# Splitting the shuffles of a long convolution into two transfers on two queues, in an H3 block with a token MLP

## The chip, the cores and the metric

The kernel runs on one core of one Trainium2 chip. The number that counts is the device time of one execution, in microseconds. Of the kernel before, three executions took 178.93, 179.75 and 180.01 us; the median is 179.75 us. A further execution, taken with the profiler, has its own time, and it is the one that the tables below describe.

The engines are TensorE (PE: matmuls and transposes, with a separate stream PEld for loading the stationary operand), VectorE (DVE), ScalarE (ACT), GpSimd (POOL) and SyncE (SP). Matmul results land in PSUM, which has eight banks here; everything else lives in SBUF, in 128 partitions. A transfer (DMA) is issued by an instruction on an engine's queue, here SP's, POOL's and a few on ACT's, and is carried out beside the engines.

## The reference

With S = 2048 positions, D = 448 channels and F = 1792 hidden units, all in bf16:

```python
h  = x + A(layernorm(x), k, v, shift_k, ssm_k, ssm_D)     # x is A_q
h2 = h + MLP(layernorm(h), w1, b1, w2, b2)

def A(q, k, v, shift_k, ssm_k, ssm_D):
    kv = shift_conv(k, shift_k) * v         # 4 taps, causal, along the positions
    y  = irfft(rfft(pad(kv)) * rfft(pad(ssm_k)))[:2048]    # along the positions, length 4096
    return q * (y + kv * ssm_D)

def MLP(x, w1, b1, w2, b2):                 # mixes positions, not channels
    u = gelu(einsum("bsd,sf->bdf", x, w1) + b1)
    return einsum("bdf,fs->bds", u, w2).transpose(0, 2, 1) + b2
```

So there is a layernorm of x, a product kv, a causal convolution of kv with a filter as long as the sequence, a gate, a second layernorm and a two-layer MLP over the 2048 positions.

## The kernel before

**Layout.** Position s is 16*q + r: q (0 to 127) lies on the partitions, r (0 to 15) in the free dimension beside the 448 channels. A tensor of the whole sequence is 128 partitions of 16 x 448 bf16 elements.

**The convolution** is done by discrete Fourier transforms written as matmuls, each transform in two stages, because a stage mixes either the partitions or the free index r. "k" stands for the filter, "u" for kv:

- *Transposes and kv* (L947, L1006 to L1028, L973, L988). The filter is transposed by PE, kv is made by PE with diagonal matrices (L973; the diagonals come from L932 on DVE, which waits for a copy L925 on POOL) and a product on DVE (L988). The tables of sines start with an angle computation on DVE, POOL and ACT (L809 to L855, with L812 and L825 on DVE and L835, L839 on POOL).
- *Stage 1* (L1040, function emit_stage1, called for k and then for u). For i in 0..3 and jh in 0..3 eight matmuls with a 128x32 stationary operand fill two PSUM banks; the result, 128 partitions x 896, is copied ("evacuated") to a slot of a ring of four buffers, by L1048 or L1050 on ACT or DVE. One slot holds one i, four jh.
- *Shuffle* (L1056). After every second jh the two finished quarters of a slot are moved between partitions, into TK or TU: source partition a + 4m + k goes to target partition a + i + 4m, so that four source partitions end side by side in one target partition. This is a DMA from SBUF to SBUF. In all there are 4 x 2 pairs for k and as many for u.
- *Stage 2* (L1075, emit_stage2), per index jj in 0..7 two blocks of 4 matmuls, each block evacuated by the helper evac (L719 and L720 on ACT, L722 and L723 on DVE; L720 and L723 are the scaled copies for k, L719 and L722 the plain ones).
- *Products* (L1108 on DVE, 16 of 128x1792) and *first inverse stage* (L1120, evacuated by L719 or L722). The first product waits for every shuffle of u, because its result lies in the memory of the ring.
- *Shuffle back* (L1144, and L1133 for the last pair), from TU to TZ: one transfer of 112 source partitions on POOL and one of 16 on SP per index; for the last pair on POOL, SP and ACT.
- *Second inverse stage* (L1240, per r) with a gate on DVE or ACT: L1249/L1251/L1259/L1269 form h from the result, the row statistics of x and x. Four transposes of a table ("ct", L1089) run between; dummy matmuls (L1154) too.

**Row statistics of x** are made on the side: bn_stats and bn_aggr on DVE (L1180, L1182), two small steps per pair of rows on POOL (L1185, L1188), normalised rows for r below 4 (L1197, L1200, then L1210 on ACT or L1212 on DVE). x itself is loaded (L896) into the ring's memory after all shuffles of u.

**The rest.** The second layernorm's statistics (L1275, L1287, L1297 to L1311) and its application (L1318 on DVE) give Q, row by row. The MLP's first layer is 112 matmuls L1365 (seven column blocks at once over 16 r, as Q comes) and 112 matmuls L1375, each block followed by a gelu (L1355 on ACT); the second layer is 16 groups of 14 matmuls (L1387), each added to h by L1390 on DVE and written out. The weights are loaded on SP (L1338, L1342, L1349) after the shuffles back.

**What sets the order.** Nothing is issued in the order of the text. Each helper call records an operation with its dependences. A list scheduler then lays the operations on the engines by a cost model, always taking, of those that are ready in the model and find a free buffer, the one with the lowest number; the numbers stand in the table WHEN, one for each step of each function (a step is one value of sch.t0). Operations that ACT or DVE could do are assigned by the table WHERE ("a" ACT, "d" DVE, "f" the scheduler's choice). PSUM banks and ring slots are also given out by this plan. The result is a fixed sequence for each engine and each queue: on the chip an engine waits at an instruction until its semaphores are there, and everything behind it on that engine waits too.

The lines that form one pair's shuffle, before:

```python
for q_, a, nu in (("pool", 0, 8), ("pool", 96, 8), ("sp", 32, 16)):
    shuf[tag].append(op(q_, lambda e, W, ...: e.dma_start(
        T[a + i:a + i + 4 * nu - 3:4]...,                      # nu target partitions, stride 4
        GR_(g.slots[0])[a:a + 4 * nu, jh - 1:jh + 1]...),      # 4 * nu source partitions
```

Of the kernel before, what the change touches and what calls it, by code (L numbers as in the profile page):

```python
# [9 lines left out]

ENGS = ("pe", "act", "dve", "pool", "sp")
WHEN = {
    "dummy": (283,),
    "tables": (138, 234, 288, 20, 81, 325, 139, 217,),
    "loads": (91, 107, 134, 143, 231, 216, 80, 297, 0, 238, 183, 285, 228, 299, 145,),
    "kv": (290, 148, 151, 174, 63, 282, 100, 192, 205, 47, 18, 112, 141, 45, 207, 160, 233,),
    "kT": (201, 13, 14, 175, 200, 130, 54, 53,),
    "k1": (132, 135, 152, 226, 122, 144, 165, 213, 68, 51, 154, 167, 89, 168, 262, 336,),
    "k2": (23, 150, 83, 97, 224, 227, 140, 153, 258, 248, 180, 195, 169, 219, 338, 235,),
    "u1": (71, 86, 116, 123, 46, 82, 176, 221, 117, 215, 261, 316, 173, 184, 277, 278,),  # L20
    "xload": (156, 298, 314, 302,),
    "bias": (75, 171,),
    "q": (271, 208, 318, 93, 268, 185, 279, 280, 264,),
    "u2": (133, 142, 220, 210, 241, 249, 64, 114, 159, 196, 137, 189, 1, 115, 252, 251,),
    "i1": (179, 121, 99, 3, 190, 96, 186, 149, 188, 240, 203, 202, 128, 92, 212, 95,),
    "ct": (36, 187, 87, 300,),
    "xn": (257, 17, 6, 222, 161, 317,),
    "w1a": (329, 239, 230, 55,),
    "w1b": (306,),
    "warm": (291, 307, 265, 27, 292, 147, 330, 320, 5, 304, 270, 38, 19, 315, 284, 62, 333, 327, 105, 118, 191, 295,  # L30
        324, 259, 56, 8, 332, 113, 236, 273, 206, 198, 182, 274,),
    "i2": (260, 69, 103, 39, 15, 31, 293, 28, 108, 242, 90, 84, 88, 331, 22, 197, 204, 33, 110, 237, 164, 323, 256,
        310, 73, 214, 223, 170, 44, 79, 157, 177, 16, 211, 328, 281, 131, 250, 4, 247, 158, 294, 109, 40, 29, 104,
        34, 243, 267, 129, 98, 287, 70, 178, 67, 162, 246, 120, 155, 2, 125, 11, 229, 42, 253, 272, 59, 124, 119,
        266, 12, 78, 194, 276, 127, 41, 313, 10, 102, 61, 255, 21, 37, 66, 24, 232, 199, 321, 312, 76, 308, 296, 52,
        111, 303, 163, 319, 58, 65, 339, 209, 26, 326, 337, 289, 85,),
    "w2": (146,),
    "mlp": (218, 57, 136, 126, 77, 30, 25, 48, 60, 9, 305, 72, 166, 245, 301, 172, 50, 181, 418, 419, 420, 421, 422,
        423, 424, 425, 426, 427, 428, 429, 430, 431, 432, 433, 434, 435, 436, 437, 438, 439,),
}  # L40
WHERE = {
    "kv": "ddaffffa",
    "kT": "fadfdddd",
    "k1": "fafaafaffaff",
    "k2": "dfdffadaafdafada",
    "u1": "fffaafadaaddafaa",
    "bias": "a",
    "u2": "fdaafafaaaaadafa",
    "i1": "affadfaaffdaffaf",
    "ct": "ffda",  # L50
    "xn": "aaff",
    "i2": "aaffaadafddf",
}


# [515 lines left out]
def _build(nc, A_q, A_k, A_v, A_shift_k, A_ssm_k, A_ssm_D, B_w1, B_b1, B_w2, B_b2, out):  # L571
# [54 lines left out]
    with ctx:  # L626
# [49 lines left out]
        def GR_(s):  # L676
            return view(o_GR[s], [R // 4, 2, D])
# [19 lines left out]
        def Ppair(b):  # L697
            s0, s1 = b.slots
            return PS[:, s0:s1 + 1, 0:D]
# [330 lines left out]
        def emit_stage1(src, o_src, T, o_T, tag):  # L1030
            shuf[tag] = []
            for i in range(R // 4):
                g = _Buf(gring)
                for jh in range(4):
                    sch.t0 = T_K1 + T_DK1 * (4 * i + jh) if tag == "k" else T_U1 + T_DU1 * (4 * i + jh)
                    b = _Buf(psum, 2)
                    c0 = 64 * (jh & 1) + 32 * (jh >> 1)
                    for x in range(2):
                        for q, r in enumerate((4 * i, 4 * i + 2, 4 * i + 1, 4 * i + 3)):
                            op("pe", lambda e, W, b=b, r=r, q=q, x=x, c0=c0: e.matmul(  # L1040
                                PS[32 * q:32 * q + 32, b.slots[x], 0:D], E[:, 2 * r + x, c0:c0 + 32], src[:, r, :],
                                start=True, stop=True, tile_position=(0, 32 * q)),
                               r=[(o_E + 512 * r + 256 * x + 2 * c0, 64), (o_src + r * DB, DB)], bw=[b], n=D, est=46.5, mode=1)

                    def fn(e, W, b=b, g=g, jh=jh, i=i):
                        dst = GR_(g.slots[0])[:, jh]
                        if tag == "k" and i == 0:
                            return e.tensor_tensor(out=dst, in0=Ppair(b), in1=DR.unsqueeze(1).broadcast_to([128, 2, D]),  # L1048
                                                   op=ALU.add)
                        return e.copy(out=dst, in_=Ppair(b)) if W == "act" else e.tensor_copy(out=dst, in_=Ppair(b))  # L1050
                    first = tag == "k" and i == 0
                    op("dve" if first else FX, fn, r=[(o_DR, DB)] if first else [], br=[b], bw=[g], n=2 * D, kind="psum")
                    if jh % 2 == 0:
                        continue
                    for q_, a, nu in (("pool", 0, 8), ("pool", 96, 8), ("sp", 32, 16)):
                        shuf[tag].append(op(q_, lambda e, W, g=g, i=i, a=a, nu=nu, jh=jh: e.dma_start(  # L1056
                            T[a + i:a + i + 4 * nu - 3:4].rearrange("p (j k) c d -> p j k c d", k=4)[:, :, jh - 1:jh + 1]
                            .rearrange("p j k c d -> p j (k c d)"),
                            GR_(g.slots[0])[a:a + 4 * nu, jh - 1:jh + 1].rearrange("p k c d -> p (k c d)")),
                           br=[g], w=[(o_T + (4 * j + jh - 1) * 2 * DB, 4 * DB, tag) for j in range(4)],  # L1060
                           dmab=4 * nu * 4 * DB, keng=nu, rate=350.0))
                wbufs.append(g)
# [296 lines left out]
        def emit_mlp():  # L1359
# [21 lines left out]
            for r in range(R):  # L1381
# [21 lines left out]

        PLAN = (("dummy", emit_dummy, ()), ("tables", emit_tables, ()), ("loads", emit_loads, ()), ("kv", emit_kv, ()), ("kT", emit_kT, ()),
                ("k1", emit_stage1, (KT, o_KT, TK, o_TK, "k")), ("k2", emit_stage2, (TK, o_TK, 1.0 / 2048.0)),
                ("u1", emit_stage1, (V, o_V, TU, o_TU, "u")),  
                ("xload", emit_xload, ()), ("bias", emit_bias, ()), ("q", emit_q, ()),
                ("u2", emit_stage2, (TU, o_TU, None)), ("i1", emit_products_i1, ()), ("ct", emit_ct, ()), ("xn", emit_xn, ()), ("w1a", emit_w1_load, (0,)), ("w1b", emit_w1_load, (1,)),
# [41 lines left out]
```

## Time and profile before

| what | value |
|---|---|
| three executions | 178.93, 179.75, 180.01 us (median 179.75) |
| the profiled execution | 178.13 us |
| its span, first to last instruction | 175.9 us |
| granted TensorE clock | 1.00 throughout |
| busy: PE, DVE, ACT, POOL | 166.1, 102.0, 92.2, 63.3 us |
| L1056 on POOL | 32 issues, 553 ns on average (median 544), 17.5 us |
| L1056 on SP | 16 issues, median 537 ns |
| L1056, from DMA to landing | 2.2 / 3.7 / 5.7 us (least, median, most) |
| L1144 on POOL | 14 issues, 588 ns on average, 8.2 us |

Some points in time of that execution, in microseconds from the start of the span:

| event | at |
|---|---|
| first L1040 of k | 13.72 |
| last stage-1 evacuation of k | 29.04 |
| last POOL shuffle of k issued, landed | 30.93, 35.90 |
| first L1075 of k | 35.99 |
| last stage-1 evacuation of u | 45.03 |
| last POOL shuffle of u issued, landed | 46.77, 50.79 |
| first, last L1108 | 50.89 start, 72.17 end |
| last evacuation of the first inverse stage | 75.17 |
| last POOL shuffle back (L1133) issued, landed | 76.30, 79.67 |
| first L1240 | 79.72 |
| first gate on DVE (L1269) | 80.31 |
| first, last L1318 | 84.80 start, 105.43 end |
| first L1365 | 85.59 |
| last matmul, end | 173.04, 175.9 |

How to read a profile: it is one execution. "Busy" is the time in which an engine had an instruction in work. The strip of 40 digits per engine shows the busy share in tenths for each fortieth of the span (4.4 us here). The chain is the sequence of work that ended last, followed back from the last instruction to whatever released it; a DMA piece there runs from the issue to the landing. A transfer's row gives the size and the median time from issue to landing. An engine's idle time matters only where the chain passes through it.

### The profile page before, as it was taken

The page shows a single profiled execution, that of the slowest core. Times are in us where ns is not written, and L with a number is a line of the kernel's source. Part 1 is how long each engine was busy: PE and PEld are TensorE (multiplying, and loading weights), DVE is VectorE, ACT ScalarE, POOL GpSimd, SP SyncE. Part 2 cuts the span into 40 slices and gives each one's busy share as a digit, 9 for nine tenths or more (in the row PEclk, how much of TensorE's full clock was granted, in tenths as well). Part 3 has the DMA queues.
Part 4 walks back from the last instruction along what each step waited for, and adds up shares of the span by engine and source line. Part 5 has one row for each costly group of instructions (what it writes and reads, how often), then busy time and mean ns, then how long its engine had stood idle before and what let it go on. Part 6 is the DMA issues. An engine that isn't in the chain of part 4 may idle for free.

```text
span 175.9 us, 3619 instructions
## 1 busy us (share of the span) xinstructions
PE 166.1 (94%) x1445; PEld 95.6 (54%) x1445; DVE 102.0 (58%) x189; ACT 92.2 (52%) x131; POOL 63.3 (36%) x157
## 2 busy tenths in 40 slices
PE   6999999879979999998999999999999999999994
PEld 2786745342323333644544455555557777777784
DVE  6995696848999999998998860000001231331331
ACT  3799958888979999966982656412120000000000
POOL 8576628670600643894888760000000000000000
PEclk9999999999999999999999999999999999999999
DMA  5999855992849386569999999910000111011111
GB/s 174 416 334 332 268 165 201 325 352 71 250 98 383 110 214 198 167 179 390 383 396 405 421 419 417 419 77 0 0 4 0 52 52 52 16 40 52 52 52 52
DMA packets 15444, 35.13 MB, mean 200 GB/s; under 512 B 3820, under 2 KB 9484, under 8 KB 15428
## 3 DMA queue, kind: packets, MB, share of 16 engines
q1 hardware_dynamic: 12164, 28.00, 43.4%
q0 software_dynamic: 3072, 6.80, 12.6%
q8 instruction: 11, 0.18, 0.4%
q10 hardware_dynamic: 192, 0.11, 0.2%
q14 instruction: 5, 0.04, 0.1%
HBM read 22.05 MB, written 1.84 MB: 136 GB/s over the span
## 4 chain that ended last, share of the span: by engine, by line
PE 68%; ACT 10%; POOL 7%; DMA 7%; DVE 4%; issue 2%; DVEq 0%; POOLq 0%
PE ps L1387 24%; PE ps L1375 12%; PE ps L1365 9%; ACT arena L719 8%; DMA arena<-arena 7%; PE ps L1040 4%; PE ps L1006 3%; POOL arena L1056 3%; PE ps L947 3%; PE ps L1240 3%; PE ps L1075 2%; PE ps L1019 2%; PE ps L973 2%; PE ps L1120 2%; DVE arena L1259 1%
## 5 line engine op out<-in xcount | busy, mean ns | idle before, releaser
L1390 DVE SCALAR_TENSOR_TENSOR arena<-ps,arena 128x448 bf16<-128x448 f32 (+2 forms) x17 | 11.1, 656 | 57.4 <-PE ps L1387 57.4
L1387 PE MATMUL ps<-arena 128*128 128x448 bf16 (+2 forms) x238 | 42.7, 342 | 0.0
L1387 PEld LDWEIGHTS ps<-arena 128*128 128x128 bf16 x238 | 33.3, 145 | 9.5
L719 ACT CAST arena<-ps 128x896 bf16<-128x896 f32 (+1 forms) x29 | 23.4, 948 | 1.2 <-PE ps L1075 1.1
L1365 PE MATMUL ps<-arena 128*128 128x448 bf16 x112 | 22.9, 353 | 0.4 <-DVE arena L1318 0.4
L1056 POOL DMA_DIRECT2D arena<-arena x32 | 17.5, 553 | 14.1 <-ACT arena L1050 12.9
L1050 ACT CAST arena<-ps 128x896 bf16<-128x896 f32 x24 | 20.3, 919 | 3.8 <-PE ps L1040 3.5
L1375 PE MATMUL ps<-arena 128*128 128x448 bf16 x112 | 21.8, 353 | 0.0
L1075 PE MATMUL ps<-arena 128*64 128x448 bf16 x128 | 15.8, 360 | 3.4 <-DMA arena<-arena 1.8
L1355 ACT ACTIVATE arena<-ps,arena 128x448 bf16<-128x448 f32 x14 | 8.6, 633 | 19.4 <-PE ps L1375 17.7
L1108 DVE TENSOR_TENSOR arena<-arena 128x1792 bf16<-128x1792 bf16 x16 | 16.7, 1080 | 0.2
L1365 PEld LDWEIGHTS ps<-arena 128*128 128x128 bf16 x112 | 10.6, 98 | 11.5 <-DVE arena L1318 2.5
L1375 PEld LDWEIGHTS ps<-arena 128*128 128x128 bf16 x112 | 10.9, 98 | 10.2
L1040 PE MATMUL ps<-arena 128*32 128x448 bf16 x256 | 15.3, 356 | 0.4 <-DVE arena L988 0.3
L1120 PE MATMUL ps<-arena 64*128 64x448 bf16 x128 | 14.0, 352 | 1.0 <-ACT arena L719 0.9
L1144 POOL DMA_DIRECT2D arena<-arena x14 | 8.2, 588 | 17.4 <-ACT arena L719 16.6
L1075 PEld LDWEIGHTS ps<-arena 128*64 128x64 f16 x128 | 5.7, 108 | 12.8 <-ACT arena L719 3.6
L1287 ACT ACTIVATE arena<-arena 128x448 bf16<-128x448 f32 x14 | 8.0, 575 | 5.9 <-DVE arena L1259 5.7
L988 DVE TENSOR_TENSOR arena<-ps,arena 128x512 bf16<-128x512 f32 (+1 forms) x16 | 9.0, 617 | 2.7 <-PE ps L973 2.7
L1120 PEld LDWEIGHTS ps<-arena 64*128 64x128 f16 x128 | 5.1, 94 | 9.5 <-ACT arena L719 5.0
L719 ACT COPY arena<-ps 128x1024 bf16<-128x1024 bf16 (+1 forms) x9 | 8.9, 1019 | 0.9 <-PE ps L1154 0.6
L1040 PEld LDWEIGHTS ps<-arena 128*32 128x32 f16 x256 | 5.1, 95 | 7.8 <-DVE arena L988 1.9
(94 smaller groups left out, 207.0 us busy)
## 6 DMA issues: line engine op xcount, KB each, us to landing
arena<-in_B_w_dram SPq DMA_DIRECT2D x8, 896.0 KB, 12.0
arena<-in_B_w_dram SPq DMA_DIRECT2D x2, 2048.0 KB, 17.1
arena<-arena SPq DMA_DIRECT2D x16, 224.0 KB, 3.7
arena<-arena POOLq DMA_DIRECT2D x32, 112.0 KB, 3.8
arena<-in_B_w_dram SPq DMA_DIRECT2D x2, 1536.0 KB, 18.7
arena<-arena POOLq DMA_DIRECT2D x14, 196.0 KB, 4.6
arena<-in_A_k_dram SPq DMA_DIRECT2D x4, 448.0 KB, 5.7
arena<-in_A_v_dram SPq DMA_DIRECT2D x4, 448.0 KB, 9.0
```

The costliest lines, as they stand in the source:

```text
L719: return e.copy(out=dst(), in_=src())
L988: return e.tensor_tensor(out=v, in0=u.rearrange("p t (r d) -> p t r d", d=64), in1=v, op=ALU.mult)
L1040: op("pe", lambda e, W, b=b, r=r, q=q, x=x, c0=c0: e.matmul(PS[32 * q:32 * q + 32, b.slots[x], 0:D], E[:, 2 * r + x, c0:c0 + 32], src[:, r ...
L1050: return e.copy(out=dst, in_=Ppair(b)) if W == "act" else e.tensor_copy(out=dst, in_=Ppair(b))
L1056: shuf[tag].append(op(q_, lambda e, W, g=g, i=i, a=a, nu=nu, jh=jh: e.dma_start(T[a + i:a + i + 4 * nu - 3:4].rearrange("p (j k) c d -> p ...
L1075: op("pe", lambda e, W, b=bs[h], h=h, j=j, c=c, par=par: e.matmul(PS[64 * par:64 * par + 64, b.slots[c], 0:D], FW[:, 64 * c:64 * c + 64], ...
L1108: op("dve", lambda e, W, m=m, i=i: e.tensor_tensor(out=MR(m.slots[0]).rearrange("p (x y) d -> p x y d", x=2), in0=TU[:, i].unsqueeze(2).br ...
L1120: k = op("pe", lambda e, W, b=bs[h], m=ms[h], par=par, t=t, tab=tab, xy=xy, P=P: e.matmul(Pb(b, par), tab[P, :], MR(m.slots[0])[P, xy, :], ...
L1365: op("pe", lambda e, W, r=r, fc=fc, b=bs[fc]: e.matmul(Pb(b), W1A[:, r, 128 * fc:128 * fc + 128], Q[:, r, :], start=(r == 0), stop=(r == R ...
L1375: op("pe", lambda e, W, r=r, fc=fc, b=b: e.matmul(Pb(b), W1B[:, r, 128 * (fc - n0):128 * (fc - n0) + 128], Q[:, r, :], start=(r == 0), sto ...
L1387: op("pe", lambda e, W, r=r, fc=fc, b=b, d0=d0, d1=d1: e.matmul(Pb(b)[:, d0:d1], W2[fc // 7][:, fc % 7, r:S:R], G[:, fc, d0:d1], start=(fc ...
L1390: op("dve", lambda e, W, r=r, b=b, A=A, d0=d0, d1=d1: e.scalar_tensor_tensor(out=X[:, r, d0:d1], in0=Pb(b)[:, d0:d1], scalar=bm[:, r:r + 1 ...
```

## The change

Each pair's shuffle becomes two transfers instead of three. Source partitions 0 to 63 go to 16 target partitions through POOL's queue, source partitions 64 to 127 to 16 target partitions through SP's. Before, POOL moved partitions 0 to 31 and 96 to 127, in two transfers, and SP moved 32 to 95. All the bytes and all their targets are the same; a POOL transfer is 224 KB instead of 112 KB, and there are 16 of them instead of 32. SP's 16 keep their size.

```diff
-                    for q_, a, nu in (("pool", 0, 8), ("pool", 96, 8), ("sp", 32, 16)):
+                    for q_, a, nu in (("pool", 0, 16), ("sp", 64, 16)):
                         shuf[tag].append(op(q_, lambda e, W, g=g, i=i, a=a, nu=nu, jh=jh: e.dma_start(
```

The second part of the change replaces both tables of the order, WHEN and WHERE, by others of the same lengths. No operation other than the shuffles is added or removed; every engine's sequence up to the MLP changes. Cut to a few rows:

```diff
 WHEN = {
-    "k1": (132, 135, 152, 226, 122, 144, 165, 213, 68, 51, 154, 167, 89, 168, 262, 336,),
-    "k2": (23, 150, 83, 97, 224, 227, 140, 153, 258, 248, 180, 195, 169, 219, 338, 235,),
-    "u1": (71, 86, 116, 123, 46, 82, 176, 221, 117, 215, 261, 316, 173, 184, 277, 278,),
+    "k1": (125, 142, 151, 175, 126, 154, 156, 206, 85, 116, 290, 291, 37, 181, 201, 204,),
+    "k2": (149, 165, 109, 124, 198, 214, 229, 237, 257, 259, 263, 274, 3, 52, 239, 260,),
+    "u1": (129, 131, 139, 150, 167, 168, 174, 193, 122, 230, 254, 261, 115, 95, 155, 161,),
...
 WHERE = {
-    "k1": "fafaafaffaff",
-    "u1": "fffaafadaaddafaa",
-    "i1": "affadfaaffdaffaf",
-    "ct": "ffda",
-    "xn": "aaff",
+    "k1": "aafdfadfdfaf",
+    "u1": "affffaaaaafffafa",
+    "i1": "ffffaafaaffafaff",
+    "ct": "aafa",
+    "xn": "aaaa",
```

What this does to the sequences, where it touches the shuffles and what follows them:

- stage-1 groups of u stand among the blocks of k's stage 2, where before 48 matmuls of u's stage 1 stood in one row; behind the last stage-1 evacuation of u, one to three evacuations of k's stage 2 are left, before eight
- L812 stands on DVE behind both L825, and so L835 and L839 on POOL come later in the sequence
- all 16 evacuations of the first inverse stage are on ACT; three of the four "ct" copies stand on ACT behind the last of them, the fourth is on DVE; the last on ACT also stands behind four L1210
- two bn_stats (L1180) stand on DVE ahead of the last product, before four; twelve stand behind it; L1212 is no longer on DVE
- on POOL the last three L1133 stand in one row, ahead of the remaining L1185 and L1188, where before these alternated
- all L1375 stand behind the L1365, where before 16 of them stood among these

## The prediction

> **What bounds the kernel now.** I read the share of each engine by slice first, then the chain that ended last, then the waits, then the DMA issues. Per slice of 4.4 us:
>
> ```profile
> PE   6999999879979999998999999999999999999994
> DVE  6995696848999999998998860000001231331331
> ACT  3799958888979999966982656412120000000000
> POOL 8576628670600643894888760000000000000000
> GB/s 174 416 334 332 268 165 201 325 352 71 250 98 383 110 214 198 167 179 390 383 396 405 421 419 417 419 77 0 0 4 0 52 52 52 16 40 52 52 52 52
> ```
>
> Two regimes are to be seen. From about slice 21 on (92 us) PE is alone: it does 448 matmuls of 448 columns (112 of L1365, 112 of L1375, 224 of L1387) at a pitch of 0.189 us, 84.5 us in all. The change leaves this work as it is; only its start can move. Between 36 and 80 us ACT and DVE are the full engines (9.84 and 8.91 us busy of the ten from 50 to 60, 9.72 and 10.00 of the ten from 60 to 70), because everything the long convolution computes leaves PSUM through them. Where they empty, they wait for the shuffles. The chain, at the two places where that happens:
>
> ```profile
> 28.25 1.53 POOL arena L1056 x3
> 29.78 0.07 issue
> 29.85 1.03 POOL arena L1056 x2
> 30.93 4.97 DMA arena<-arena
> 35.90 0.09 issue
> 35.99 0.96 PE ps L1075 x8
> ...
> 45.70 1.07 POOL arena L1056 x2
> 46.77 4.02 DMA arena<-arena
> 50.83 0.99 PE ps L1075 x8
> ...
> 75.67 0.62 POOL arena L1133
> 76.30 3.37 DMA arena<-arena
> 79.72 1.69 PE ps L1240 x8
> ```
>
> Columns are start, length, piece. The POOL queue issues six small shuffles in a row, the last at 30.93 although its data was evacuated at 29.04, and PE, ACT and DVE stand until it has landed; the same at 46.77 (data ready at 45.03) and, for the shuffle back, at 76.30 (data ready at 75.17, POOL busy with L1188 between). The price list of the transfers:
>
> ```profile
> arena<-arena SPq DMA_DIRECT2D x16, 224.0 KB, 3.7
> arena<-arena POOLq DMA_DIRECT2D x32, 112.0 KB, 3.8
> arena<-arena POOLq DMA_DIRECT2D x14, 196.0 KB, 4.6
> ```
>
> **Issue.** A POOL issue of L1056 takes 0.544 us (median of 32), one of L1144 0.588 for 112 pieces: size hardly enters. So 32 issues become 16, 8.7 us less of POOL. Most of that lies beside waiting; it counts where issues stand in a row at the end of each half, six each time. SP keeps 16 issues of 0.537 us and 224 KB, with other partitions.
>
> **Landing.** Not in the trace: 64 source partitions of one half into 16 targets from POOL. Bounds by row: an SP shuffle of 224 KB alone landed 2.2 us after its issue (26.41 to 28.61), a POOL one of 112 KB alone 2.4 and 2.9 (26.68, 43.70); the worst of all 48 took 5.7; a slope through POOL's 112 and 196 KB (3.8, 4.6) gives 4.9 at 224 KB. I take 3.6 for the last k shuffle, still part of a burst (SP's row of the same size, 3.7, is nearest), and 2.85 for the last u shuffle, which the new order leaves nearly alone. The other ends are R1 and R3 below.
>
> [...]
>
> **The path, step by step** (before → after; the after column is a walk through the new order of each engine with the durations of these rows: evacuation of 128x896 at a pitch of 0.80 us on ACT and 1.0 on DVE, so 0.44 for one when both work; product L1108 1.0; BNStats 0.52; aggregation 0.08):
>
> 1. *Start.* First k stage-1 group 13.72 → about 13.2. On POOL the angle work L835/L839 (3.96 us, 8.21 to 12.17) now follows L812 behind both L825 on DVE, so it ends about 14.3; L925 (0.18) and L932 on DVE follow at 16.9 instead of 17.30. It is covered by about 2.4 us; if every L835 takes the 2.17 us of its first instance (the others took 0.36), L932 comes 1.2 late and all after it. Last k evacuation 29.04 → 28.9.
> 2. *Last k shuffle issued* 30.93 → 29.5 (three POOL issues in the row for six save 1.6; a little is lost to the order). *Landed* 35.90 → 33.1. Stage 2 of k starts 2.8 earlier, but with three k1/u1 evacuations (1.35) still undone that before had behind it: net −1.5.
> 3. *Last u stage-1 evacuation* 45.03 → 45.9. It is later because u's groups now stand among the blocks of k's stage 2, of which one to three remain behind instead of eight: 5.5 x 0.44 = 2.4 us of work done earlier, less the 1.5.
> 4. *Last u shuffle issued* 46.77 → 45.95 (nothing queued ahead on POOL), *landed* 50.79 → 48.8, first product 50.89 → 49.6 (DVE finishes evacuations first; the products wait for all u shuffles, whose ring they overwrite).
> 5. *Last product* 72.17 → 68.05. Of the 4.1: 1.3 from the start; 1.3 from three evacuations more done before; 1.0 from two BNStats fewer ahead of the products; 0.5 from L1212, which leaves DVE.
> 6. *Last evacuation of the inverse* 75.17 → 70.15: the 4.1, and one copy of 1.03 us (73.33 to 74.36) that no longer stands ahead on ACT.
> 7. *Last shuffle back issued* 76.30 → 70.7, three L1133 in one row on POOL and L1185/L1188 behind them; landed after the same 3.4: 79.67 → 74.1.
> 8. *First gate on DVE* 80.31 → 76.3. Here the gain shrinks: 12 BNStats now stand behind the last product, 12 x 0.60 with their aggregation plus one copy of about 1 us, 68.05 + 8.2. DVE, not the landing, is late by 2.2 us.
> 9. *First L1318* 84.80 → 80.7, *first L1365* 85.59 → 81.25. The W1 loads wait for the shuffles back and move with them (first landed 82.03, 3.6 us before use; 5 earlier by step 7). PE after that gives back about 0.2, since all of L1375 follows 58 L1365 without the interleaving of before.
>
> Sum: −4.1. The profiled execution took 178.13 (span 175.9 and 2.2 around it), so 174.0; the median of the runs shown, 179.75, stands 1.6 above it, so **175.6**. A measurement of this kernel tells about 1%, 1.8 us, from no change.
>
> **Rivals.**
>
> R1, *the burst lands as now.* A 4.97 us landing after 29.5 and 4.02 after 45.95 give 34.5 and 50.0, 1.35 and 1.2 late against the walk; ACT and DVE work in a fixed order, so both add: −1.6, 178.1. For it: 325 and 352 GB/s in slices 7 and 8, bytes unchanged, so fewer transfers need not land sooner. Against: half of the wait at 30.93 was the queue of issues, which is gone.
>
> R2, *the gain is won and eaten behind the products.* Step 8 leaves 2.2 us between landing and gate. In the new order PE's third L1240 block waits for a PSUM bank freed by the last ct copy, which stands on ACT behind four L1210; if this stall (1.8 us by the walk) and a BNStats pass at its 0.62 duration (12 x 0.1 = 1.2) are not hidden in one another, −4.1 becomes −1.1; about 178.7. With step 1's 1.2 as well, nothing is left: no change.
>
> R3, *slower: a transfer from one half lands late.* Place: the last k and the last u shuffle. Price: each microsecond of landing costs one at each place, since ACT and DVE have nothing else that their order allows. It decides from 2.05 us over the walk at each (5.7 us and 4.9 us from issue), where the 4.1 are used up. At 3 us more, about twice the present isolated landing, the time is +1.9: 181.6. For it: POOL's 112 KB pieces now use eight engines for 0.55 us; if one of 224 KB still uses eight, that is 1.1 us, and pieces queue behind each other. Against: the sum of bytes is the same, and 5.7 is the worst of 48 landings now.
>
> R4, *the change does not do what it says.* The order shows 16 L1056 on POOL for 32, so this is only that the walk's order of milestones fails; it is within R2.
>
> **How the numbers follow.** The walk, −2.9 to −6.0: 0.45; R1, −1 to −2.9: 0.19; R2 and R4, −1.8 to +1: 0.15; R3, +1 and more: 0.19; better than −6.0 (172 to 173.7), if the landings are those of isolated ones: 0.02. The range reaches from below the walk to a R3 of +1.3: 173.4 to 181.0, leaving out about 0.15; the walk's own range is 173.7 to 176.8. Faster by over 1% takes the walk and most of R1, 0.63; within 1% 0.18; slower 0.19.
>
> **What would show it.** L1056 on POOL at x16 with about 0.55 us each; landings of L1056 (3.7 median now) at or under 3.7: right; over 5: R3. First L1075 near 33.2, first L1108 near 49.6, last L1108 near 68, the first L1240 near 74 to 76, first L1365 near 81.3. If the chain shows DVE BNStats and not a DMA before the first gate, step 8 is right. I am wrong if the first L1365 comes after 84.5, or if PE stands idle between 92 us and the end, where now it does not.

## The result and the profile after

The change made the kernel slower: 181.51 us (180.92 to 181.87) against 179.43 us (178.93 to 180.01), a ratio of 1.0148, 95% interval 1.0099 to 1.0196. That is a small loss, but one clear of no change. The forecast was 175.6; even its range ended at 181.0. (Now and then an execution of the same kernel is slower by one per cent or more; ratios here leave such executions out, and from two profiles below that are of such ones, of the order of after with three transfers and of the run with added matmuls, only lengths of single pieces are read.) The profiled execution took 181.56, with a span of 179.7; it is this execution that "after" stands for in times and lines below.

The same strips of the profile after, one digit for 4.5 us:

```profile
PE   6999969839999999999999989999999999999994
ACT  3597847828999999977885844421211000000000
POOL 8006433220120259696586880000000000000000
PEclk9999999978999999999999999999999999999999
DMA  6998944996375965673999999980000111011111
GB/s 190 396 336 309 281 139 148 254 245 182 104 219 142 363 200 173 198 208 94 395 383 404 410 416 421 417 368 8 0 4 0 51 51 47 4 55 51 51 51 51
```

POOL is emptier, as it should be: its L1056 went from 17.5 us to 8.4. But PE and ACT have a hole at the ninth digit (3 and 2), and there and at the tenth the granted clock, 1.00 throughout before, is 0.7 and 0.8. At the eighth and ninth digit the transfer engines are full (9, 9) but move 254 and 245 GB/s, where before they moved 325 and 352.

From the chain of after, the places that answer to those shown of before (start, length, piece):

```profile
19.87 5.94 DMA arena<-arena
25.96 0.91 ACT arena L1050
...
31.22 6.40 DMA arena<-arena
37.61 1.10 issue
38.72 3.06 PE ps L1075 x16
...
56.36 1.09 DVE arena L1108
...
77.03 5.96 DMA arena<-arena
83.00 0.09 issue
83.09 0.55 PE ps L1240 x2
83.66 1.28 DVE arena L1269 x2
```

Two of its transfers are longer than their counterparts (6.40 for 4.97, 5.96 for 3.37), and one stands at a place that before's chain did not have: at 19.87, where an evacuation of stage 1 waits for a slot of the ring until a shuffle out of it has landed. The "issue" of 1.10 belongs to the wait of PE that follows: the L1075 needs POOL's shuffle issued at 31.48 too, and that landed at 38.51. And 16 L1075 take 3.06 us, where before eight took 0.96.

The wait of ACT for landings (in all, times, longest), the prices in the profile's DMA rows, and the spread of all 32 landings, after:

```profile
ACT arena L1050 <- DMA arena<-arena: 3.0, 2, 2.4
arena<-arena SPq DMA_DIRECT2D x16, 224.0 KB, 5.2
arena<-arena POOLq DMA_DIRECT2D x16, 224.0 KB, 5.6
DMA to landing us min/median/max: 3.1/5.4/8.0
```

Before, the 48 landed after 2.2 / 3.7 / 5.7 us (least, median, most). SP's transfers kept their size and number; only their partitions changed, and they too went from 3.7 to 5.2.

### The profile page after: what moved, and what is told of

Its sections match the earlier page's. It is cut to its first block, busy times and chain, and to the rows that moved or that the text cites. A ratio compares the mean times of both kernels' runs of the same rounds, so it can differ in the third digit from the quotient of the medians.

```text
span 179.7 us, 3584 instructions
## 1 busy us (share of the span) xinstructions
PE 167.3 (93%) x1445; PEld 97.2 (54%) x1445; DVE 102.9 (57%) x190; ACT 91.6 (51%) x130; POOL 51.6 (29%) x141
## 4 chain that ended last, share of the span: by engine, by line
PE 56%; DVE 18%; DMA 10%; ACT 6%; POOL 6%; issue 3%; DVEq 0%; ACTq 0%; POOLq 0%
PE ps L1387 23%; PE ps L1375 12%; DMA arena<-arena 10%; DVE arena L1108 8%; PE ps L1365 5%; ACT arena L1050 4%; PE ps L1040 4%; PE ps L1006 3%; PE ps L1075 3%; PE ps L1019 2%; DVE arena L722 2%; PE ps L947 2%; POOL arena L1311 2%; DVE arena L1318 2%; DVE arena L1269 1%
## 5 line engine op out<-in xcount | busy, mean ns | idle before, releaser
L1050 ACT CAST arena<-ps 128x896 bf16<-128x896 f32 x25 | 21.5, 910 | 6.4 <-PE ps L1040 3.3
L719 ACT CAST arena<-ps 128x896 bf16<-128x896 f32 x28 | 23.2, 970 | 0.4
L1365 PE MATMUL ps<-arena 128*128 128x448 bf16 x112 | 22.7, 353 | 0.8 <-DVE arena L1318 0.8
L1375 PE MATMUL ps<-arena 128*128 128x448 bf16 x112 | 21.4, 352 | 0.0
L1075 PE MATMUL ps<-arena 128*64 128x448 bf16 x128 | 17.1, 385 | 4.0 <-issue 3.3
L1040 PE MATMUL ps<-arena 128*32 128x448 bf16 x256 | 15.3, 356 | 2.5 <-ACT arena L1050 2.0
L1365 PEld LDWEIGHTS ps<-arena 128*128 128x128 bf16 x112 | 10.7, 98 | 11.6 <-DVE arena L1318 2.2
L1375 PEld LDWEIGHTS ps<-arena 128*128 128x128 bf16 x112 | 11.0, 98 | 10.2
L1108 DVE TENSOR_TENSOR arena<-arena 128x1792 bf16<-128x1792 bf16 x16 | 16.4, 1083 | 0.1
L1056 POOL DMA_DIRECT2D arena<-arena x16 | 8.4, 528 | 26.8 <-ACT arena L1050 23.5
L1120 PE MATMUL ps<-arena 64*128 64x448 bf16 x128 | 14.1, 351 | 0.9 <-ACT arena L719 0.4
L1075 PEld LDWEIGHTS ps<-arena 128*64 128x64 f16 x128 | 6.6, 116 | 14.0 <-issue 6.6
L723 DVE TENSOR_SCALAR arena<-ps 128x896 bf16<-128x896 f32 x9 | 9.5, 1088 | 5.6 <-PE ps L1075 5.6
L1144 POOL DMA_DIRECT2D arena<-arena x14 | 8.4, 602 | 12.7 <-ACT arena L719 12.7
L719 ACT COPY arena<-ps 128x1024 bf16<-128x1024 bf16 (+1 forms) x8 | 8.0, 1016 | 4.6 <-PE ps L1019 3.5
L1040 PEld LDWEIGHTS ps<-arena 128*32 128x32 f16 x256 | 5.1, 95 | 9.1 <-ACT arena L1050 3.7
```

The lines of the kernel that those rows point to most:

```text
L719: return e.copy(out=dst(), in_=src())
L723: return e.tensor_scalar(out=dst(), in0=src(), scalar1=scale, scalar2=None, op0=ALU.mult)
L1040: op("pe", lambda e, W, b=b, r=r, q=q, x=x, c0=c0: e.matmul(PS[32 * q:32 * q + 32, b.slots[x], 0:D], E[:, 2 * r + x, c0:c0 + 32], src[:, r ...
L1075: op("pe", lambda e, W, b=bs[h], h=h, j=j, c=c, par=par: e.matmul(PS[64 * par:64 * par + 64, b.slots[c], 0:D], FW[:, 64 * c:64 * c + 64], ...
L1108: op("dve", lambda e, W, m=m, i=i: e.tensor_tensor(out=MR(m.slots[0]).rearrange("p (x y) d -> p x y d", x=2), in0=TU[:, i].unsqueeze(2).br ...
L1120: k = op("pe", lambda e, W, b=bs[h], m=ms[h], par=par, t=t, tab=tab, xy=xy, P=P: e.matmul(Pb(b, par), tab[P, :], MR(m.slots[0])[P, xy, :], ...
```

## The experiments

The two tables of the order are read by a scheduler, so that changing the transfers alone would also change the order. To keep them apart, the plan made for one kernel (each engine's sequence, the PSUM banks and the ring's slots) was written down and replayed with other transfers. Every engine's sequence is then the same but for the shuffles themselves. The edit in short:

```diff
-for q_, a, nu in (("pool", 0, 16), ("sp", 64, 16)):
+for q_, a, nu in (...):                 # the transfers of the run
...
+_Sched.schedule = _replay               # plays back the plan of before or of after
```

**The order of after, the three transfers of before.**

> The sequence of every engine exactly as in the kernel after, but each pair's shuffle as the three transfers of before (POOL 0 to 31 and 96 to 127, SP 32 to 95). Theory H (a transfer whose 64 source partitions lie in one half is moved at about half the rate, and this alone made the change slow): median landing of L1056 back from 5.4 to about 3.7 us, first L1108 near 51, time 175 to 178 us, faster than before. Rival O (the new order is what costs): 180.5 to 182, as after. Rival S (POOL transfers of 224 KB are slow whatever their partitions): the same as H here.

Ratio to before 1.0025 (0.9981 to 1.0068): neither the gain of H nor the loss of O. The landings fell as theory H has it, to 3.0 us in the median, so the transfers are what made 1.0148 out of this; but the order had no gain left. The trace showed a possible reason on POOL that the walk did not have. POOL's and DVE's timelines (start, length, what):

```profile
61.37 1.17 POOL L1144 DMA_DIRECT2D arena<-arena  x2 [2.07 <-ACT arena L719]
62.61 3.23 POOL L1185 TENSOR_SCALAR arena<-arena 128x2 f32<-128x2 f32 x1
65.92 0.72 POOL L1188 TENSOR_TENSOR arena<-arena 128x2 f32<-128x2 f32 x1
66.60 1.27 POOL L1144 DMA_DIRECT2D arena<-arena  x2
67.87 1.14 POOL L1197 TENSOR_TENSOR arena<-arena 128x2 f32<-128x2 f32 x1
```

```profile
61.68 4.07 DVE L1108 TENSOR_TENSOR arena<-arena 128x1792 bf16<-128x1792 bf16 x4
65.87 1.09 DVE L722 CAST arena<-ps 128x896 bf16<-128x896 f32 x1
66.88 3.09 DVE L1108 TENSOR_TENSOR arena<-arena 128x1792 bf16<-128x1792 bf16 x3
```

The L1185, 0.24 us elsewhere, was held for 3.23 and ended at 65.84, when the row of four products on DVE ended (65.75). Eight of the 14 L1144 and the three L1133 stand behind it on POOL's queue. Whether that is what ate the gain is tested further down.

**The order of after, POOL moving the middle.**

> The sequence of after, but POOL moves partitions 32 to 95 in one transfer of 224 KB, and SP moves 0 to 31 and 96 to 127 in two of 112 KB. H: POOL's transfer now draws on both halves, landings near 3.7 us, 175.5 to 178.5. S: POOL's landings stay at 5 to 6 us, 180 to 182. O: 180.5 to 182.

Its four executions lay too far apart for a verdict on the time (178.67 to 181.94). The landings do tell the theories apart. POOL's four transfers of 224 KB in the quiet stretch at the end of u landed after 2.9, 2.3, 2.3 and 2.5 us, those of after in the same places of the sequence after 3.8, 3.5, 3.5 and 3.6. Same queue, same size, same number of targets: the partitions differ, and with them what SP moves beside it. S falls. Over all 16 the gain is smaller, 4.1 us in the median for 5.6, and not the 3.7 of H:

```profile
arena<-arena POOLq DMA_DIRECT2D x16, 224.0 KB, 4.1
```

**The order of before, the two transfers.**

> The sequence of before exactly, with the two transfers of after (POOL 0 to 63, SP 64 to 127; each stands where POOL's first and SP's one stood). H: landings of L1056 of 5 us or more, first L1108 1 to 3 us later than 50.9, time 181 to 184. O: 178.5 to 180, no slower than before, since 16 POOL issues of 0.54 us are gone. S: as H.

1.0102 (1.0059 to 1.0146), 180.39 us: slower, by a little less than the least that H expected, with landings of 3.1 / 5.5 / 8.2 us. First L1108 at 52.47, 1.6 later than before. O falls: in before's own order, with 16 POOL issues fewer, the two transfers cost 1.0%.

**Transfers one at a time.**

> The kernel before with eleven SBUF-to-SBUF transfers of the shuffle's shape added behind the last matmul of L1365, one at a time, each waiting for the one before it to land, into memory that is dead by then; the result is the reference's. H: on SP, partitions 0 to 63 and 64 to 127 land 0.4 to 0.6 us later than 32 to 95 (about 2.2); on POOL, 0 to 63 and 64 to 127 land 0.4 to 0.6 later than 32 to 95, which lands like the 112 KB of 0 to 31 (2.4). S: on SP the three are alike, and on POOL all of 224 KB land about 0.5 us or more after the 112 KB. One transfer of all 128 partitions (448 KB) about 1.1 us of packets by H, landing near 2.8.

| from | queue | KB | landed after, us |
|---|---|---|---|
| 32 to 95 | SP | 224 | 2.26 |
| 0 to 63 / 64 to 127 | SP | 224 | 2.65 / 2.69, 2.72 |
| 0 to 31 | POOL | 112 | 2.29 |
| 32 to 95 | POOL | 224 | 2.13 |
| 0 to 63 / 64 to 127 | POOL | 224 | 2.54, 2.58 / 3.68 |
| 0 to 127 | SP / POOL | 448 | 2.86 / 2.75 |

(The 2.26 stood beside POOL's two; SP's first one alone ran into the weight loads and is left out.) One half costs 0.4 us more than the middle on either queue, as H expected; the single 3.68 is not explained. From POOL, 224 KB out of the middle land no later than 112 KB. And 448 KB of all partitions land only 0.1 to 0.2 after 224 KB of one half. The targets of a piece lie in the same part of the partitions as its sources, so no run tells which side costs.

**Transfers in a row.**

> The kernel before with groups of transfers of the shuffle's shape added behind L1365, into dead memory; each group moves four pairs (1.79 MB) at once and waits for the group before: three transfers a pair as before, two a pair as after, one a pair of all 128 partitions on SP, then three, two, and one on POOL; the result is the reference's. H (a transfer within one half runs at half the rate): the group of two a pair takes from first issue to last landing 1.5 us or more longer than that of three. Against H (only a fixed delay a transfer): at most 0.5 longer. One a pair: the shortest or equal to three, if both halves at once is what counts.

From first issue to last landing: three a pair 9.2 us, two a pair 9.9, one a pair 6.5 on SP and 6.9 on POOL. (A second group of three took 9.1 and of two 10.1; beside these and both groups of one, output writes were under way.) The difference of three and two, 0.7, is not the 1.5 that H wanted, nor the 0.5 at most of its rival. The eight POOL issues of the three are spread over 4 us, and from the last issue it is 5.0 against 7.8; but in the middle of the groups the rates are alike, 260 and 245 GB/s, with 406 for one a pair and some output beside it. So in a dense row of four pairs the three-way form is itself slow, against H; that its advantage lies where pairs come less densely, as in the kernel, is my reading and was not varied. What stands out is the form that neither kernel uses.

**After, with matmuls into the hole.**

> The kernel after, its sequences unchanged, with 14 matmuls without use ahead of the first L1075 of k, where PE stands 3.3 us and then runs at a granted clock of 0.51 to 0.64 until 42. Theory C (about 1.2 us of the loss is the clock that falls when PE stands over some 3 us): the first 16 L1075 take 1.9 us instead of 3.06, the clock of the execution is 1.00 or one dip higher than after, time 179.8 to 180.8, 0.7 to 1.7 less than after. Rival (the matmuls only wait for data, the clock costs nothing): within 0.4 of after's 181.5.

```profile
35.34 2.84 PE ps L1161 x14
38.18 0.50 issue
38.68 0.96 PE ps L1075 x8
```

The mechanism is there: the L1075 behind the added matmuls take 0.96 for eight again, and the clock from 38 to 42 us is 1.00. In the time nothing can be told: 1.0142 (1.0055 to 1.0229) cannot be set apart from after's 1.0148, but the interval is wider than the 0.6% in question. So the 1.1 us of the clock (3.06 for 16 against twice 0.96) are a size seen in the trace, not a gain shown in time.

**The held steps moved.**

> The sequence of after with the three transfers of before, and on POOL the first L1185, L1188, L1197, which stood between the L1144 and took 3.2, 0.7 and 1.1 us there with DVE full of products, moved behind the last L1133 (with the L1200 on DVE that needs them). Theory T (these steps hold up the shuffles back, and so the gain upstream is lost): L1144 issued when their data are ready, L1133 landed by about 78.5, first gate at D + 8.6, time 176.5 to 178, faster than before. Rival (the shuffles back are late because they come in a row, whatever stands between): landings of L1133 5 to 7 us as now, 178 to 180.

The edit of POOL's sequence in short (on DVE, one L1200 moves with it):

```diff
 POOL's sequence
 L1144 x6
-L1185, L1188
 L1144 x2
-L1197
 L1144 x6
 L1133 x3
+L1185, L1188, L1197
```

0.9984 (0.9954 to 1.0014). The barrier came as T expected (first L1240 at 77.75, before 79.72), but my own edit put a wait in its place: DVE stood 2.0 us at the L1200 that needs these steps, with eight BNStats behind it, and the first gate was at 80.28. So the next run moved that L1200 further back:

> As the run with the sequence of after, three transfers and the first L1185, L1188, L1197 behind the last L1133, but with the L1200 that needs them moved to the other L1200, since in that run DVE stood 2.0 us at it. Theory T (with fast landings and nothing in the way, the new order has the gain that the walk saw behind the last product: first gate at D + 8.2): D near 70, first gate near 78.3, first L1365 near 83.5, time 176 to 177.3, ratio to before 0.984 to 0.992. Rival (the order is worth nothing whatever stands in the way): ratio 0.995 to 1.002.

176.93 us, 0.9924 (0.9886 to 0.9961): faster than before, and faster than the first run with this order, from which only four small steps were moved. T stands: the order has a gain, and it needed these four steps out of the way. Its size is at the small end of what T expected (first gate at D + 9.0, first L1365 at 84.00).

**After itself with the same four steps moved.**

> The kernel after, with only the first L1185, L1188, L1197 and L1200 moved as in the two runs beside this. H: what the two transfers cost in this order, without the chance of a held L1185, shows as the difference to the run with three: D 3 to 5 us later (74.9 for 70), time 179.5 to 181.5. Rival (most of after's loss was the held POOL steps): 177 to 178.5.

180.8 us, 1.0123 (1.0072 to 1.0175). Beside the 0.9924 of the run above, the two transfers cost 2.0% in this order, twice what they cost in before's. The rival falls.

**One transfer a pair.** The probes' best form, in before's order, twice:

```diff
-for q_, a, nu in (("pool", 0, 8), ("pool", 96, 8), ("sp", 32, 16)):
+for q_, a, nu in (("sp", 0, 32),):
```

> The sequence of before with one transfer of all 128 partitions on SP for each pair (448 KB, 16 issues) and none on POOL. By H nothing is lost against the three: both halves are used at once; landings near 3.5 in a burst and 2.9 alone, and the row of six POOL issues is gone, so 176.5 to 179. Rival (one queue's transfers of this size follow each other): landings over 5 us, 180 or more.

> The sequence of before with one transfer of 128 partitions on SP for each pair, once more beside the others. If its gain is real: ratio 0.983 to 0.996 again; if the first interval was luck: 0.995 to 1.005.

0.9897 (0.9826 to 0.9968) and 0.9900 (0.9833 to 0.9967), 176.64 and 176.77 us: faster. The first L1108 stands at 50.43 in the second run although stage 1 began 0.5 late. The stretches of the DMA burst for k, in the profile's table by stretch (last two columns: share of time in which the 16 transfer engines are busy, GB/s; the one before them is the granted clock). Before:

```profile
32.00:34.00 2.00, 2.00 (x48) 0.81 (x43) 1.50 (x4) 1.80 (x3) 0.74 (x2) 1.00 1.03 321
34.00:36.00 2.00, 0.56 (x14) 0.15 (x7) 1.54 (x2) 1.47 (x2) 1.89 (x4) 1.00 0.95 377
```

After:

```profile
34.00:36.00 2.00, 1.42 (x28) 0.37 (x24) 1.87 (x4) 1.51 (x2) 0.76 (x2) 1.00 1.08 251
36.00:38.00 2.00, 0.00 (x0) 0.00 (x0) 0.67 (x1) 0.91 (x1) 1.26 (x3) 1.00 1.00 242
38.00:40.00 2.00, 1.28 (x8) 0.83 (x10) 0.00 (x0) 0.00 (x0) 0.00 (x0) 0.51 1.09 265
40.00:42.00 2.00, 2.00 (x18) 1.07 (x15) 1.29 (x2) 1.15 (x2) 0.00 (x0) 0.64 0.99 255
```

One transfer a pair, before's order:

```profile
30.00:32.00 2.00, 2.00 (x49) 1.05 (x39) 1.14 (x3) 1.84 (x3) 0.00 (x0) 1.00 1.02 405
32.00:34.00 2.00, 2.00 (x48) 1.07 (x48) 1.50 (x4) 2.00 (x3) 0.00 (x0) 1.00 0.98 380
```

The transfer engines are full in all of them, and move about 350, 250 and 390 GB/s: the same bytes to the same places, cut into other pieces. In after the packets themselves take longer: those of 3584 bytes (SP's) took 0.15 us in the mean before, 0.23 after (both from 32 to 36 us) and about 0.15 with one transfer (worked out from the share and the rate in the last two rows). In the probe with transfers one at a time, SP's packets of one half took 0.19 us in the mean (26.3% of 16 engines over 2.9 us, for 64 of them), where those of the middle, landing alone in before, had 0.14. POOL's packets of 7168 bytes took 0.27 from the middle in the probe (23.9% over 2.3 us, for 32) and 0.28 in the 112 KB piece of one half that before issues at 26.68; so it is 64 partitions within one half that are slow here, and not every piece within a half. In the dense rows of the burst probe, three and two a pair were alike in this too (about 0.2 for SP's packets in both, one a pair 0.15). For one against three, the 32 issues that POOL no longer makes are a second possible cause, which no run separates.

**And in the new order:**

> The same with one transfer of all 128 partitions on SP for each pair. If the two gains (one transfer: 1.0% in the order of before; the order: as in the run beside this) add: 174.5 to 176.5, faster than both kernels. Rival: landing is no longer what stands last there, so the same as the run with three, 176 to 177.5.

175.84 us, 0.9849 (0.9778 to 0.9920): faster than both kernels. The product of the two gains (0.990 and 0.9924) lies within the interval.

| ratio to before | three | two | one |
|---|---|---|---|
| order of before | 1 | 1.0102 | 0.990 |
| order of after | 1.0025 | 1.0148 (the change) | not run |
| order of after, four steps moved | 0.9924 | 1.0123 | 0.9849 |

## Why the prediction was wrong

The points of the walk, from the trace of each (us from the start of the span; D is the end of the last product). The start of stage 1 lay between 12.9 and 15.0 in the profiled executions, whatever the transfers were, so it stands first:

| | before | walk | after | before's order, two | after's order, moved, three | the same, one |
|---|---|---|---|---|---|---|
| first L1040 of k | 13.7 | 13.2 | 14.1 | 13.4 | 13.7 | 13.3 |
| first L1075 of k | 35.99 | 33.15 | 38.72 | 37.43 | 35.02 | 33.89 |
| last evacuation of u | 45.0 | 45.9 | 52.3 | 46.5 | 47.4 | 46.3 |
| first L1108 | 50.89 | 49.6 | 56.36 | 52.47 | 51.30 | 50.17 |
| D | 72.17 | 68.05 | 74.85 | 73.80 | 69.93 | 68.81 |
| first gate on DVE | 80.31 | 76.3 | 83.66 | 81.63 | 78.91 | 77.79 |
| first L1365 | 85.59 | 81.25 | 88.95 | 86.91 | 84.00 | 82.88 |
| the execution's time | 178.13 | 174.0 | 181.56 | 179.15 | 176.78 | 175.66 |

**The step that failed is the landing (step 2; step 4's was low too, but hidden).** I took 3.6 us for the last k shuffle "part of a burst", from SP's row of the same size. That row was of transfers from 32 to 95, which use both halves. Measured: issued at 31.48, landed at 38.51, 7.0 us; so 3.4 of the 5.6 us by which the first L1075 came later than walked are the landing, and 2.0 the later issue. The last of u took 3.6 us for 2.85, in the quiet. The size was bounded from the wrong row: the bounds went by KB, and KB was not what mattered. By the prediction's own signs it is wrong and R3 holds: the landings are over 5 in the median, and the first L1365 came after 84.5. R3 had the sign, and one of its two places: k. I gave it 0.19, and argued it away by "the sum of bytes is the same", which does not settle it: the sum of bytes was the same and the rate fell by three tenths.

That R3's 181.6 is so near the 181.51 measured is luck. It takes 3 us more at both places; at u the landing was 0.7 over the walk, and hidden: it came at 56.19, when DVE still had an evacuation until 56.30, and the first product stands behind that. Step 4 says as much (landed 48.8, first product 49.6, evacuations first), and R1 and R3 both leave these 0.8 us out of their sums. What R3 lacked, a ring and the clock, follows below.

One at a time, 64 partitions within one half land 0.4 us after the middle (2.65 to 2.72 us for 2.26 on SP); in the kernel's burst 250 GB/s stand for 350. At the two places of R3 the 0.4 would come to 0.8 us, an estimate. Counted from the start of stage 1, the two transfers cost 4.5 us at D in after (60.8 against 56.3, where the order is that of after but for the four moved steps), and 3.8 where those steps are moved as well (60.1), because in the burst it is a rate and not a delay, and because it is paid in more places than those two. Why a piece within one half is slower, no run shows. In the order of before, one transfer of all 128 partitions stands at 0.990 and two of disjoint halves at 1.0102.

**A place that the walk lacked.** The ring of four slots is shared by k and u. An evacuation that needs a slot waits for the shuffles out of it, so a late landing also stops the evacuations: the L1050 at 25.96 in after ends an idle time of ACT of 2.4 us that only the landing set. With three transfers and the four steps moved its counterpart ended at 25.1 instead of 26.9, stage 1 having begun 0.4 earlier. This run also splits the bill. Its last k shuffle was issued at 30.39 and landed after 4.4 us. So of the 4.9 us by which D is later in after (74.85, 69.93), 0.4 are the start, 0.7 the later issue behind the ring, 2.6 the landing itself, and 1.2 come between the first L1075 and the last evacuation of u; the rest is nothing. Of the 1.2, 1.1 are the first 16 L1075 at the low clock, since PE stood 3.3 us (before: 1.4, at a clock of 1.00 throughout). In before's order the two transfers cost 1.4 us at the first L1075 and 1.4 still at the last evacuation of u: PE stood 3.0 us there, and the clock stayed at 1.00. That accounts for part of why they cost twice as much in the new order. Two of after's four executions had a mean clock of 0.981, where the profiled one has 0.991; at the same depth that would be a clock low for about twice as long, an estimate from the two means; no profile of this kernel shows the place.

**The other steps.** Step 1 was right in that L835 began late (POOL waited 8.8 us for L812) and L932, at 17.28, was covered. But stage 1 began at 14.1 and not 13.2, and the last k evacuation came at 31.2 and not 28.9, behind the ring's wait. Step 3's direction was right, later, but by 7 us with the landing in it. Step 5 from the first product on was right to 0.1: 18.49 us from the first L1108 to D, against 18.45 in the walk and 21.28 before. Step 6 too (last evacuation D + 2.0, walk 2.1). Step 7 was too low: the three L1133 on POOL landed after 5.3 us, not 3.4, and the barrier came at D + 8.2 and not D + 6.05. They are the last of seven POOL issues within 4.5 us (73.55 to 78.07); that this is the reason is argued, not shown. Step 8 was right in size (D + 8.8, walk 8.25), but by its own sign it fails: the chain has a DMA and not BNStats before the first gate, though these ended only just before the landing (82.94, 82.99), so the size is partly luck. With three transfers and the four steps moved it holds as written: the first L1240 is at 77.70, and DVE's last steps set the gate at 78.91. Step 9: first L1365 5.3 after the gate (walk 4.95), and PE gave back 0.4 behind it (walk 0.2).

**R1 and R2.** With three transfers, and once the four steps are moved, the order is worth what R1 gave it, not what the forecast did: 1.35 us of gain in the profiled executions (178.13 to 176.78), 1.6 by R1. The landing there is 4.4 us, and the last k issue 0.9 later than walked; with u's landing counted in full in R1, the agreement is closer than its reasons. R2's stall at the third L1240 decided nothing in after: DVE, not PE, was last. But "eaten behind the products" was true in another place, the held L1185, which no row of before could show: there, all L1185 stand behind the last product. That the new sequence puts three such steps among the products was visible, and I did not price it. In after itself it was not the main loss: with these steps moved and the two transfers kept, the ratio is still 1.0123.

## What to carry to other kernels

Before cutting a transfer into other pieces, look at which partitions each piece draws on, and not only at its size: bound its cost from rows of the same partitions, and as a rate where several are under way. Where there is no such row, a probe of single transfers gives one. If a shuffle touches all partitions, one transfer of all 128 was best here, on one queue, with half as many issues as the change had (0.990 of before's time in its order, 0.9849 in the new one). And when an order is changed, look at what each wait holds besides the next instruction: a ring slot, the clock of an engine that stands idle, and a small step on a queue that has transfers behind it.

## What the runs showed of the hardware that I had not expected

- A POOL step on 2 elements a partition, 0.24 us long elsewhere, took 3.23 us while DVE ran products of 128x1792 without a gap, and ended within 0.1 us of their end; in the run with added matmuls the same step took 3.46. It is not so in every execution: in the profile of after this step took 0.38, and the L1188 behind it 1.41, 0.70 elsewhere. With three transfers, the ratio to before was 0.9924 with these steps out of the products and 1.0025 with them among these.
- After 3.3 us without a matmul, TensorE's granted clock was 0.51 over 2 us and 0.64 over the next 2; after 1.4 us it was 1.00. Near 3 us the length alone does not decide: PE stood 3.0 us in the run with before's order and two transfers (34.44 to 37.43) and as long in the one of after with the four steps moved (34.32 to 37.33), and the clock (the third number from the end) stayed in the first and fell in the second:

```profile
36.00:38.00 2.00, 0.57 (x7) 0.45 (x9) 0.00 (x0) 1.48 (x2) 0.23 (x1) 1.00 1.01 283
38.00:40.00 2.00, 1.75 (x20) 0.92 (x16) 1.09 (x1) 1.58 (x2) 0.78 (x2) 1.00 1.03 269
```

```profile
36.00:38.00 2.00, 0.67 (x4) 0.42 (x6) 0.00 (x0) 0.05 (x1) 0.34 (x1) 0.63 0.98 244
38.00:40.00 2.00, 2.00 (x14) 1.05 (x10) 0.93 (x1) 0.92 (x1) 0.00 (x0) 0.51 1.00 249
```

- One transfer of 448 KB over all partitions landed, alone, 0.1 to 0.2 us after one of 224 KB from one half, and in the burst for k ran at 380 to 405 GB/s.
